# Weight splits of the first and last steps of a fused attention and GeGLU kernel placed elsewhere in the step order

## The chip, the cores and the metric

The kernel runs on one core of one Trainium2 chip, in one launch. Its time is the device time of that core in microseconds (us). Three runs of the kernel before took 1610.37, 1612.19 and 1613.04 us, with 1612.19 us as the median. Traces come from one profiled execution each.

## The reference

The input x has 2048 tokens of 576 elements. Two branches read it, and a gate of its own per token mixes them.

```python
x = A_x
g = _sigmoid((x * gate_w).sum(-1, keepdims=True))
a = _A_ref(x, A_wq, A_wk, A_wv, A_wo, A_beta)   # 32 heads of 18, 4 segments of 512 tokens
b = _B_ref(x, B_w_gate, B_w_up, B_w_down)       # (gelu(x @ w_gate) * (x @ w_up)) @ w_down
return g * a + (1 - g) * b
```

Branch A is attention with a compressive memory: within each segment of 512 tokens a causal softmax attention, mixed head by head with a read of a memory that the earlier segments wrote, and an output projection by wo (576 x 576). Branch B is a gated feed-forward layer with 4608 hidden units: w_gate and w_up are 576 x 4608, w_down is 4608 x 576. All of it is in float32.

## The kernel before

Every float32 product is made of fp16 matmuls: an operand is scaled by a power of two and split into a high half (a cast by ScalarE) and a low half (the operand minus its high half, by GpSimd or VectorE). Three products high-high, high-low and low-high stand for one.

The kernel has three stages. The first (to about 228 us of the profile) projects q, k and v, keeps the attention memory and writes q, k, v and the memory's result to DRAM. The second is a hand-made order of 72 steps, `step(v)` for v = 0 to 71, each about 18 us in the profile. The third adds the last down products and the output projection to the result, row block by row block.

A step has two jobs. Its own job is feed-forward work: step v treats hidden tile f = v // 2 (128 of the 4608 units) and token pair p = v % 2 (two of the four segments). With sums of weights and of inputs, kept as tiles pairg and xt, it forms gate and up products in few matmuls: `product` and `rest` (lines 1039, 1046 and 1051) accumulate in three PSUM banks named V (bank V), X (bank G) and Y (bank U). VectorE copies and adds between banks (L1141, L1144, L1176, L1195, L1203), ScalarE applies gelu (L1029), VectorE multiplies by the up value (`hidden`, L1021, which empties banks G and U), and ScalarE and GpSimd split the hidden value in two halves hh (L1025, L1026). Two tiles make a block fb = v // 4, and i4 = v % 4. The down products of block fb - 1 (`down`, L999, six matmuls and one VectorE accumulation L1005 or L1007) are spread over the four steps of block fb: eight chains per step, five early and three late. They take turns in two PSUM banks named dn. Block 0 (v = 0 to 3) has no down products to fill in; its first products are issued a step ahead instead.

The other job is attention. A unit is one head in one segment; scores of unit a go to banks st and dn (`scores`, L902), VectorE adds the mask and takes maxima (L910), ScalarE exponentiates (`powers`, L920, L923) and casts the high rows (`pair_rows`, L933), GpSimd forms the low rows (L934), and the DMA queue of SyncE transposes high and low rows (`turn_rows`, L940). `values` (L954) multiplies the transposed rows by v, and `normalize` follows. Attention lags by LAG = 2: step v scores units 2k and 2k + 1 with k = v - 2, and takes the values of two units of the step before. The transposed rows pt have two buffers, the values of a head one bank.

The weights of a coming tile are prepared beside this: loads of gate and up weights into one of three buffers raw (L196) and of down weights into one of two buffers rawd (L202), scaling on GpSimd (`scale_g`, L264, two pieces a tile; `scale_d`, L303), sums on GpSimd (`sums_g`, L285 to L289), and the split: `high_g(f, b)` on ScalarE (L295), `low_g(f, b)` on GpSimd (L299), with b = 0 before the sums and b = 1 after them, and `high_d`, `low_d` (L307, L311) for the down weights. From block 1 on `weights_first`, `weights_high` and `weights_low` place these; in block 0 single lines of `step` do.

At the end, from step LAST = 67 on, `finish(i)` prepares the output weights: i = 0 loads five pieces of wo, i = 1 takes their squares on ScalarE, i = 2 sums those on TensorE (L90, into a bank dn), derives the scale by short VectorE operations (L104, L97, L76, L77, L99, L100) and scales the gate (L1269), and i = 2, 3 and 4 split pieces 0 and 1, 2 and 3, and 4 (high half on ScalarE, L108; low half on VectorE, L111).

The order on TensorE, ScalarE, VectorE and GpSimd is the order in which the code issues instructions; each engine works through its own in turn and waits by semaphores. The order on SyncE's DMA queue is chosen by the framework; it too is worked through in turn, and a DMA that must wait for a buffer holds up those behind it.

Of the kernel before, what the change touches and what calls it, by code (L numbers as in the profile page):

```python
# [42 lines left out]
def kernel(ctx: ExitStack, tc: tile.TileContext, xs, wqk, wv, wo, wgu, wd, beta, out):  # L43
# [215 lines left out]
    def scale_g(f):  # L259
        if f >= NF:  # L260
            return
        for i in (1, 0):
            r = raw_g[f][:, i * KW : (i + 1) * KW]
            pool.tensor_scalar(r, r, scl[f // 2][0][:, 0:1], None, OP.mult)  # L264
# [26 lines left out]
    def high_g(f, b):  # L291
        if f < NF and not b:
            pair_g[f] = wts.tile([P, 2, GB * P], F16, name="pairg", tag="pairg", bufs=2)
        for p in parts_g(f, b):
            act.activation(spot(f, *p, 0), raw_g[f][:, p[0] : p[1]], AF.Copy)  # L295

    def low_g(f, b):
        for p in parts_g(f, b):
            pool.tensor_tensor(spot(f, *p, 1), raw_g[f][:, p[0] : p[1]], spot(f, *p, 0), OP.subtract)  # L299

    def scale_d(f):
        r = raw_d[f]
        pool.tensor_scalar(r, r, scl[f // 2 + 1][0][:, 1:2], None, OP.mult)  # L303

    def high_d(f):
        t = pair_d[f] = home["d"].tile([P, 2, D], F16, name="paird", tag="paird", bufs=4)
        act.activation(t[:, 0], raw_d[f], AF.Copy)  # L307

    def low_d(f):
        t = pair_d[f]  # L310
        pool.tensor_tensor(t[:, 1], raw_d.pop(f), t[:, 0], OP.subtract)  # L311
# [535 lines left out]
    with tc.tile_pool(name="keep", bufs=2, side="right", reuse_waits="tile") as kp, ExitStack() as tail:  # L847
# [270 lines left out]
        def step(v):  # L1118

            f, p = divmod(v, 2)  # L1120
            fb, i4 = divmod(v, 4)
            c, e = 2 * p, 2 * p + 1
            k = v - LAG
            on = lambda i: 0 <= i < 2 * H
# [6 lines left out]
            low = (k - 6) // 4 if i4 == 0 and 0 <= (k - 6) // 4 < H // 2 - 1 else None  # L1131
            x1, x2_, t = x16[c], x16[e], xt[p]
            end_pair()
            if v == 3:
                high_g(2, 1)
                low_g(2, 1)
            act_squares(v)
            V = ahead.pop(v) if v in ahead else first_product(v)
            X, Y = bank("G"), bank("U")
# [7 lines left out]
            if v == 1:  # L1147
                scale_result()
            some(fb - 1, early[:1])
            put(2 * k - 1, 1)  # L1150
            put(2 * k - 1, 2)
            puts.pop(2 * k - 1, None)
# [1 line left out]
                values(2 * k - 3)  # L1154
            weights_first(fb, i4)
            if v == 1:
                scale_d(0)
                scale_d(1)
            if on(k - 1):
                powers(2 * k - 1)  # L1160
                pair_rows(2 * k - 1, 0)
# [32 lines left out]
                puts[2 * k] = scores(2 * k)  # L1194
            dve.tensor_tensor(g1, Y, g1, OP.add)  # L1195
            gelu(f, e, g1, g1)
            if v == 3:
                for n in range(2):
                    high_d(n)
                    low_d(n)  # L1200
            put(2 * k, 2)
            if fb:
                dve.tensor_tensor(g0, V, g0, OP.add)  # L1203
                gelu(f, c, g0, g0)
            if on(k - 1) and fb:
                values(2 * k - 2)
            some(fb - 1, early[3:4])
            put(2 * k, 0)
# [6 lines left out]
                hidden(f, c, X, g0)  # L1215
                hidden_pair(f, c, g0)
            if v == 0:
                scale_g(2)
            if on(k):
                powers(2 * k)  # L1220
                pair_rows(2 * k, 0)
# [7 lines left out]
            if low is not None:  # L1229
                result_low(low)  # L1230
            some(fb - 1, late[1:])
            if on(k - 1) and not fb:
                values(2 * k - 2)
            if fb:
                low_rests(f, (X, U4, x1), (Y, UG, x2_))
# [20 lines left out]
        def finish(i):  # L1256

            if i == 0:
                for k in range(KT):
                    rows[k] = op_.tile([P, D], F32, name="wor", bufs=5)  # L1260
                    sp.dma_start(rows[k], wo[:, k])
            if i == 1:
                for k in range(KT):
                    wos[k] = op_.tile([P, 2, D], F16, name="wo", bufs=5)
                    act.activation(wos[k][:, 1].bitcast(BF16), rows[k], AF.Square, accum_out=wst[:, k : k + 1])
            if i == 2:
                scale_sum(2, wst[:, 0:5])

                dve.tensor_scalar(gate[:, 2], gate[:, 0], wis[:, 2:3], wis[:, 3:4], OP.mult, OP.mult)  # L1269
            if i >= 2:  # L1270
                for k in ((0, 1), (2, 3), (4,))[i - 2]:
                    pair_of(wos[k], rows[k], wsc[:, 2:3])

        LAG = 2
        LAST = 2 * H + LAG + 1
        with tc.manual_schedule(engines=ORDERED):
            for v in range(2 * NF):
                step(v)

                if v == LAST:  # L1280
                    atn.close()
                    op_ = tail.enter_context(tc.tile_pool(name="outp", bufs=2, side="right", reuse_waits="tile"))
                if v >= LAST:
                    turned(2 * (v - LAST))
                    turned(2 * (v - LAST) + 1)
                    finish(v - LAST)
            end_pair()
            turns.update(of=3)


            fb = NB - 1
            for t in range(10, 16):
                turned(t)
            for t in range(16):
                for n in range(2):
                    down(fb, t, n)
                for n in range(2):
                    o = bank("st", 2)
                    chain_x(o[:, :NH], lambda i: ot[t][:, i], lambda k, b: wos[k][:, b, n * NH : (n + 1) * NH])
                    av = acc[:, t, n * NH : (n + 1) * NH]  # L1300
                    dve.scalar_tensor_tensor(av, o[:, :NH], gate[:, 2, t : t + 1], av, OP.mult, OP.add)
                    if t == 15:
                        sp.dma_start(out[t * P :, n * NH : (n + 1) * NH], av)
                if t < 15:
                    sp.dma_start(out[t * P : (t + 1) * P, :], acc[:, t])
# [40 lines left out]
```

## Time and profile before

| | us |
|---|---|
| median of three timed runs | 1612.19 |
| lowest and highest run | 1610.37, 1613.04 |
| span of the profiled execution, first to last instruction | 1608.8 |
| TensorE (PE) busy | 1594.9 |
| ScalarE (ACT) busy | 1162.3 |
| VectorE (DVE) busy | 1141.2 |
| GpSimd (POOL) busy | 1132.9 |

The profiled execution is known by its span; the median of the timed runs is 3.4 us longer. Rows of a timeline read: start in us from the span's start, duration in us, engine, line, operation, output and input tiles with shapes, count, and in brackets the idle time of the engine before the instruction with what ended it. Rows of a group read: busy us and mean ns, then idle us before them. Rows by stretch read: length, then busy us (and instructions) of PE, PEld, DVE, ACT and POOL, the granted clock of TensorE, the busy share of the DMA engines and GB/s. Lines are those of the kernel before.

### The profile page before, as it was taken

To read this page: it belongs to the slowest core of one execution; us is meant where nothing else is said; L and a number is where in the kernel's file an instruction comes from. 1 tells how busy PE (TensorE), PEld (TensorE's weight loads), DVE (VectorE), ACT (ScalarE), POOL (GpSimd) and SP (SyncE) were. 2 spreads that over 40 slices of the span, in tenths; PEclk is the share of its full clock that TensorE was granted. 3 is DMA by queue.
4 is the path that set the end of the run, shared out by engine and by line. 5 is a ranking of instruction groups with operands and counts; after the bars stand their busy time and mean duration, and the time that the engine had idled before them with its cause. 6 is when DMAs were issued, how large, how long until landed. Compare 5 with 4: busy or idle time off the path is not lost.

```text
span 1608.8 us, 32608 instructions
## 1 busy us (share of the span) xinstructions
PE 1594.9 (99%) x11924; PEld 933.3 (58%) x11924; DVE 1141.2 (71%) x2938; ACT 1162.3 (72%) x1968; POOL 1132.9 (70%) x1093
## 2 busy tenths in 40 slices
PE   9999999999999999999999999999999999999999
PEld 6655754555555555555555555555555555555577
DVE  6575785677777777777777777777777777765543
ACT  6666446888888888888888888888888888863200
POOL 2233647798978888888978788887879787885200
PEclk9999999999999999999999999999999999999999
DMA  6532343788878788888987898878788797837251
GB/s 243 190 122 81 133 146 85 122 139 126 136 122 141 123 142 125 142 136 126 141 128 136 126 145 124 145 123 155 130 132 135 130 136 129 129 65 166 49 133 60
DMA packets 472016, 209.00 MB, mean 130 GB/s; under 512 B 427568, under 2 KB 437040, under 8 KB 471344
## 3 DMA queue, kind: packets, MB, share of 16 engines
q1 hardware_dynamic: 471856, 206.92, 71.1%
q8 instruction: 94, 1.54, 0.4%
q14 instruction: 66, 0.54, 0.1%
HBM read 90.99 MB, written 27.26 MB: 73 GB/s over the span
## 4 chain that ended last, share of the span: by engine, by line
PE 96%; DMA 1%; DVE 1%; POOL 1%; ACT 0%; issue 0%; SPq 0%; POOLq 0%; DVEq 0%
PE dn L999 26%; PE U L1039 17%; PE V L1039 12%; PE G L1039 11%; PE pv L954 4%; PE st L328 3%; PE st L318 3%; PE dn L328 2%; PE G L318 2%; PE U L1046 2%; PE st L902 2%; PE V L1051 1%; PE U L318 1%; PE G L1051 1%; PE V L1046 1%; PE G L1046 1%
## 5 line engine op out<-in xcount | busy, mean ns | idle before, releaser
L934 POOL TENSOR_TENSOR ph<-pf,ph 128x512 f16<-128x512 f32 (+1 forms) x256 | 354.0, 1404 | 177.8 <-ACT ph L933 175.9
L999 PE MATMUL dn<-paird,hh 128*128 128x288 f16 x3396 | 476.8, 286 | 0.9 <-POOL paird L311 0.9
L1039 PEld LDWEIGHTS <-pairg 128*128 128x128 f16 x3024 | 285.0, 98 | 312.6 <-issue 17.6
L999 PEld LDWEIGHTS <-hh 128*128 128x128 f16 x3456 | 332.3, 98 | 138.1 <-issue 2.6
L1007 DVE SCALAR_TENSOR_TENSOR acc<-dn,ev,acc 128x288 f32<-128x288 f32 x534 | 274.0, 516 | 95.9 <-PE dn L999 87.2
L923 ACT ACTIVATE pf<-pf,mb,esc 128x512 f32<-128x512 f32 (+3 forms) x512 | 292.9, 642 | 6.7
L1039 PE MATMUL G<-x,pairg 128*128 128x512 f16 x864 | 209.9, 379 | 4.0 <-DVE gl L1021 4.0
L1039 PE MATMUL U<-xt,pairg 128*128 128x512 f16 x864 | 210.0, 379 | 0.0
L1026 POOL TENSOR_TENSOR hh<-gl,hh 128x512 f16<-128x512 f32 x144 | 163.9, 1159 | 56.1 <-ACT hh L1025 56.1
L910 DVE CUSTOM_DVE_ANT_0 pf<-st,mask 128x512 f32<-128x512 f32 (+2 forms) x384 | 183.9, 504 | 0.0
L299 POOL TENSOR_TENSOR pairg<-raw,pairg 128x640 f16<-128x640 f32 (+2 forms) x144 | 173.9, 1230 | 10.6 <-ACT pairg L295 10.6
L933 ACT ACTIVATE ph<-pf 128x512 f16<-128x512 f32 (+1 forms) x256 | 172.4, 720 | 0.0
L1176 DVE COPY gl<-U 128x512 f32<-128x512 f32 x72 | 49.8, 691 | 135.6 <-PE U L1039 135.6
L295 ACT ACTIVATE pairg<-raw 128x640 f16<-128x640 f32 (+2 forms) x144 | 89.5, 648 | 69.9 <-POOL raw L289 40.7
L264 POOL TENSOR_SCALAR raw<-raw,sc 128x640 f32<-128x640 f32 x72 | 134.8, 1885 | 0.0
L1029 ACT ACTIVATE gl<-gl,sc 128x512 f32<-128x512 f32 x144 | 98.3, 717 | 45.9 <-DVE gl L1195 25.5
L1039 PE MATMUL V<-xt,pairg 128*128 128x512 f16 x432 | 105.7, 381 | 0.0
L1195 DVE TENSOR_TENSOR gl<-U,gl 128x512 f32<-128x512 f32 x72 | 49.7, 690 | 78.6 <-PE U L1051 71.3
L1039 PE MATMUL U<-x,pairg 128*128 128x512 f16 x432 | 105.0, 379 | 0.4 <-DVE gl L1195 0.4
L1039 PE MATMUL V<-x,pairg 128*128 128x512 f16 x432 | 104.8, 378 | 0.4 <-ACT hh L1025 0.2
L1025 ACT ACTIVATE hh<-gl 128x512 f16<-128x512 f32 x144 | 82.8, 616 | 24.9 <-DVE gl L1021 24.8
L920 ACT ACTIVATE mb<-mx,esc 128x4 f32<-128x4 f32 x128 | 37.8, 295 | 86.5 <-DVE mx L910 83.7
(268 smaller groups left out, 2566.6 us busy)
## 6 DMA issues: line engine op xcount, KB each, us to landing
raw<-in_wgu_dram SPq DMA_DIRECT2D x36, 640.0 KB
rawd<-in_wd_dram SPq DMA_DIRECT2D x36, 288.0 KB
qk<-stage SPq DMA_DIRECT2D x36, 256.0 KB
qt<-qk SPq DMA_DIRECT2D x128, 72.0 KB
kt<-qk SPq DMA_DIRECT2D x128, 72.0 KB
vp<-vstage SPq DMA_DIRECT2D x16, 296.0 KB
vt<-vp SPq DMA_DIRECT2D x16, 296.0 KB
qt<-qk SPq DMA_DIRECT2D x128, 36.0 KB
```

Source lines behind the costliest of these rows:

```text
L264: pool.tensor_scalar(r, r, scl[f // 2][0][:, 0:1], None, OP.mult)
L299: pool.tensor_tensor(spot(f, *p, 1), raw_g[f][:, p[0] : p[1]], spot(f, *p, 0), OP.subtract)
L318: pe.matmul(o, w(k, a), x[:, 4 * b + k], start=n == 0, stop=False)
L910: dve.tensor_tensor_reduce(prob[a][:, COL[qi] : COL[qi + 1]], ov, mask[:, L - (qi + 1) * P :], 1.0, -3e38, OP.add, OP.max, mx[a][:, qi : q ...
L923: act.activation(r, r, AF.Exp, bias=b[:, qi : qi + 1], scale=esc[:, 0, c : c + 1])
L933: act.activation(h[:, 0, cols], p[:, cols], AF.Copy)
L934: pool.tensor_tensor(h[:, 1, cols], p[:, cols], h[:, 0, cols], OP.subtract)
L999: pe.matmul(o[:, :NH], hh[:, a, q * P : (q + 1) * P], w[:, b, n * NH : (n + 1) * NH], start=i == 0, stop=i == 5)
L1007: dve.scalar_tensor_tensor(av, o[:, :NH], ev, av, OP.mult, OP.add)
L1026: pool.tensor_tensor(hh[:, 1], t, hh[:, 0], OP.subtract)
L1029: act.activation(t, o, AF.Gelu_apprx_tanh, scale=scl[f // 2][0][:, 2 + c : 3 + c])
L1039: pe.matmul(o, w[:, i, (a + k) * P : (a + k + 1) * P], x[:, b + k], start=start and k == 0 and i == 0 and b == h, stop=k == 1 and i == 1, ...
```

## The change

Five things are placed elsewhere; no computation is added or left out.

- The scaling of the first two down weight tiles (`scale_d(0)`, `scale_d(1)`) moves from v = 1 to the end of v = 0. Their splits (`high_d`, `low_d`) move from v = 3 to v = 1. The scaling of the third gate and up tile (`scale_g(2)`) moves from the end of v = 0 to v = 1, behind them.
- The second half of that tile's split (`high_g(2, 1)`, `low_g(2, 1)`) moves from the start of v = 3 to v = 2, behind the gelu of the second token segment.
- The even values of v = 4 (`values(2)`, of unit 2) move from behind the scores of unit 4 to behind the late down chains of the step. From v = 5 on they stay where they were.
- `finish(2)`, `finish(3)` and `finish(4)` move from the ends of v = 69, 70 and 71 to the same steps' first third, behind the first early down chain.

```diff
@@ step(v)
-            if v == 3:
-                high_g(2, 1)
-                low_g(2, 1)
             act_squares(v)
...
             some(fb - 1, early[:1])
+            if v >= LAST + 2:
+                finish(v - LAST)
             put(2 * k - 1, 1)
...
             if v == 1:
-                scale_d(0)
-                scale_d(1)
+                for n in range(2):
+                    high_d(n)
+                    low_d(n)
+                scale_g(2)
...
             gelu(f, e, g1, g1)
-            if v == 3:
-                for n in range(2):
-                    high_d(n)
-                    low_d(n)
+            if v == 2:
+                high_g(2, 1)
+                low_g(2, 1)
...
-            if on(k - 1) and fb:
+            if on(k - 1) and v > 4:
                 values(2 * k - 2)
...
             if v == 0:
-                scale_g(2)
+                scale_d(0)
+                scale_d(1)
...
-            if on(k - 1) and not fb:
+            if on(k - 1) and v <= 4:
                 values(2 * k - 2)
@@ behind step(v)
-                    finish(v - LAST)
+                    if v < LAST + 2:
+                        finish(v - LAST)
```

What this does to GpSimd's order in v = 0 and v = 1, from the split of the first hidden value on (raw is the third tile, rawd and paird the two down weight tiles). Before:

```order
L1026 TENSOR_TENSOR hh_2521<-gl,hh_2521 128x512
L264 TENSOR_SCALAR raw<-raw,sc 128x640 x2
L882 MEMSET ob 128x288
L1026 TENSOR_TENSOR hh_2550<-gl,hh_2550 128x512
L303 TENSOR_SCALAR rawd<-rawd,sc 128x576 x2
L1026 TENSOR_TENSOR hh_2621<-gl,hh_2621 128x512
```

And now:

```order
L1026 TENSOR_TENSOR hh_2521<-gl,hh_2521 128x512
L303 TENSOR_SCALAR rawd<-rawd,sc 128x576 x2
L882 MEMSET ob 128x288
L1026 TENSOR_TENSOR hh_2550<-gl,hh_2550 128x512
L311 TENSOR_TENSOR paird<-rawd,paird 128x576 x2
L264 TENSOR_SCALAR raw<-raw,sc 128x640 x2
L1026 TENSOR_TENSOR hh_2627<-gl,hh_2627 128x512
```

The scaling of the down weights has taken the place of that of the third tile, and the latter comes behind the down weights' low halves.

GpSimd's order in v = 2 and v = 3, from the last of the third tile's sums on (ph are the low rows of attention units 0 and 1, pairg the third tile's second half). Before:

```order
L289 TENSOR_TENSOR raw<-raw 128x128
L1026 TENSOR_TENSOR hh_2726<-gl,hh_2726 128x512
L934 TENSOR_TENSOR ph<-pf,ph 128x512
L934 TENSOR_TENSOR ph<-pf,ph 128x768
L1026 TENSOR_TENSOR hh_2771<-gl,hh_2771 128x512
L299 TENSOR_TENSOR pairg<-raw,pairg 128x640
L299 TENSOR_TENSOR pairg<-raw,pairg 128x512
L934 TENSOR_TENSOR ph<-pf,ph 128x512
L934 TENSOR_TENSOR ph<-pf,ph 128x768
L311 TENSOR_TENSOR paird<-rawd,paird 128x576 x2
L1026 TENSOR_TENSOR hh_2867<-gl,hh_2867 128x512
```

And now:

```order
L289 TENSOR_TENSOR raw<-raw 128x128
L299 TENSOR_TENSOR pairg<-raw,pairg 128x640
L299 TENSOR_TENSOR pairg<-raw,pairg 128x512
L1026 TENSOR_TENSOR hh_2736<-gl,hh_2736 128x512
L934 TENSOR_TENSOR ph<-pf,ph 128x512
L934 TENSOR_TENSOR ph<-pf,ph 128x768
L1026 TENSOR_TENSOR hh_2781<-gl,hh_2781 128x512
L934 TENSOR_TENSOR ph<-pf,ph 128x512
L934 TENSOR_TENSOR ph<-pf,ph 128x768
L1026 TENSOR_TENSOR hh_2867<-gl,hh_2867 128x512
```

Between the low rows of unit 0 and those of unit 1 only one hidden value is left, and none of the weights' low halves stand in v = 3. ScalarE's high halves have moved in the same way. On the DMA queue the load of the sixth tile, which needs the third tile's buffer, now stands ahead of the loads of head 2 and of the transposes of unit 0, where it stood behind the latter; the loads of the second pair of down weights stand some twenty places further ahead.

VectorE's order at v = 69. Before, from the last five down accumulations of the step to the two products that follow it:

```order
L1007 SCALAR_TENSOR_TENSOR acc<-dn,ev,acc 128x288 x5
L104 TENSOR_REDUCE sv<-dn 128x1
L97 TENSOR_SCALAR wz<-sv 128x1
L76 TENSOR_SCALAR va<-wz 128x1
L77 TENSOR_SCALAR va<-va 128x1
L99 TENSOR_SCALAR wsc<-va 128x1
L100 TENSOR_SCALAR wis<-va 128x1
L1269 TENSOR_SCALAR gate<-gate,wis 128x16
L111 SCALAR_TENSOR_TENSOR wo<-wor,wsc,wo 128x576 x2
L1021 SCALAR_TENSOR_TENSOR gl<-G,sc,gl 128x512
L1021 SCALAR_TENSOR_TENSOR gl<-U,sc,gl 128x512
```

And now, from the first early down chain's accumulation on (L1177 and L1270 are the former L1176 and L1269):

```order
L1007 SCALAR_TENSOR_TENSOR acc<-dn,ev,acc 128x288
L104 TENSOR_REDUCE sv<-dn 128x1
L97 TENSOR_SCALAR wz<-sv 128x1
L76 TENSOR_SCALAR va<-wz 128x1
L77 TENSOR_SCALAR va<-va 128x1
L99 TENSOR_SCALAR wsc<-va 128x1
L100 TENSOR_SCALAR wis<-va 128x1
L1270 TENSOR_SCALAR gate<-gate,wis 128x16
L111 SCALAR_TENSOR_TENSOR wo<-wor,wsc,wo 128x576 x2
L1177 COPY gl<-U 128x512
L1007 SCALAR_TENSOR_TENSOR acc<-dn,ev,acc 128x288
```

The chain of the output weights no longer stands ahead of the two L1021 that empty banks G and U for the next step, but ahead of the copy of bank U in the middle of its own.

## The prediction

> **What bounds the kernel now.** I read the page first, then the waits of TensorE, then TensorE's busy time by stretch, and only then the instructions of the two stretches that are not full.
>
> ```profile
> span 1608.8 us, 32608 instructions
> PE 1594.9 (99%) x11924; PEld 933.3 (58%) x11924; DVE 1141.2 (71%) x2938; ACT 1162.3 (72%) x1968; POOL 1132.9 (70%) x1093
> ```
>
> TensorE is occupied in all but 13.9 us of the span. The change removes no matmul, so it can only win what TensorE waits. The two longest waits of TensorE (total us, times, longest us):
>
> ```profile
> PE G L1039 <- DVE gl L1021: 4.0, 3, 2.7
> PE pv L954 <- DMA pt<-ph: 3.4, 4, 1.5
> ```
>
> The stretches say where they lie (us, then TensorE busy):
>
> ```profile
> 200.00:300.00 100.00, 94.89 (x537) 47.41 (x536) 67.20 (x156) 59.43 (x97) 61.82 (x57) 1.00 0.47 115
> 1450.00:1500.00 50.00, 46.98 (x279) 26.14 (x277) 28.94 (x60) 17.84 (x34) 23.38 (x26) 1.00 0.75 172
> ```
>
> 5.1 us are lost in the stretch of the steps v = 0 to 4, 3.0 us in that of v = 68 to 70: over half of the 13.9 us, and the places of the change. The granted clock (the third number from the end) is 1.00 in both rows.
>
> **The head: v = 3 and v = 4.** TensorE's own instructions, from the first product of v = 4 to that of v = 6:
>
> ```profile
> 275.08 1.47 PE L1039 MATMUL V<-xt,pairg 128*128 128x512 f16 x6
> 278.14 0.53 PE L999 MATMUL dn<-paird,hh 128*128 128x288 f16 x3 [0.17 <-POOL paird L311]
> 279.37 0.40 PE L999 MATMUL dn<-paird,hh 128*128 128x288 f16 x2 [0.71 <-POOL paird L311]
> 280.61 0.64 PE L954 MATMUL pv<-vt,pt 128*128 128x37 f16 x19 [0.81 <-DMA pt<-ph]
> 290.73 0.19 PE L954 MATMUL pv<-vt,pt 128*128 128x37 f16 x1 [1.53 <-DMA pt<-ph]
> 291.84 0.64 PE L954 MATMUL pv<-vt,pt 128*128 128x37 f16 x19 [0.92 <-DMA pt<-ph]
> 298.29 1.47 PE L1039 MATMUL V<-xt,pairg 128*128 128x512 f16 x6
> 316.78 1.47 PE L1039 MATMUL V<-xt,pairg 128*128 128x512 f16 x6
> ```
>
> Step v = 4 takes 298.29 - 275.08 = 23.21 us, step v = 5, which runs the same instructions, 18.49 us: v = 4 is 4.7 us too long. The named waits make 4.14 us of it: 0.88 for the low half of the first down weights (L311), 0.81 for the values of unit 1, 2.45 for those of unit 2.
>
> The rows that feed these waits: the group of L264 on the page (busy us, mean ns), then instructions of GpSimd, ScalarE and the DMA queue:
>
> ```profile
> L264 POOL TENSOR_SCALAR raw<-raw,sc 128x640 f32<-128x640 f32 x72 | 134.8, 1885 | 0.0
> ```
> ```profile
> 245.40 3.42 POOL L303 TENSOR_SCALAR rawd<-rawd,sc 128x576 f32<-128x576 f32 x2
> 259.36 0.45 POOL L289 TENSOR_TENSOR raw<-raw 128x128 f32<-128x128 f32 x1
> 271.27 2.53 POOL L299 TENSOR_TENSOR pairg<-raw,pairg 128x640 f16<-128x640 f32 x2
> 276.81 2.51 POOL L311 TENSOR_TENSOR paird<-rawd,paird 128x576 f16<-128x576 f32 x2 [0.30 <-ACT paird L307]
> ```
> ```profile
> 252.63 1.13 ACT L295 ACTIVATE pairg<-raw 128x640 f16<-128x640 f32 x2
> 262.41 0.63 ACT L1025 ACTIVATE hh<-gl 128x512 f16<-128x512 f32 x1 [1.58 <-DVE gl L1021]
> 268.51 1.24 ACT L295 ACTIVATE pairg<-raw 128x640 f16<-128x640 f32 x2
> 272.17 1.35 ACT L933 ACTIVATE ph<-pf 128x512 f16<-128x512 f32 x2
> ```
> ```profile
> 276.54 2.10 SPq L940 DMA_TRANSPOSE pt<-ph  x1
> ```
>
> *Down weights in v = 1.* Their scaling (3.42 us) moves to v = 0, and the low halves (2.51 us of GpSimd) now stand where it stood, at 245.40: they end near 247.9 us, 30 us before TensorE first uses them. The 0.88 us go, and would come back only if they were 30 us late. What they push is the scaling of the third tile, now behind them: two pieces of 1.885 us, done near 251.7. ScalarE takes that tile at 252.63. Margin 0.9 us, so I cost it at nothing; without it each us goes on to the next paragraph.
>
> *Third tile's second half in v = 2.* Its sums end at 259.36 + 0.45 = 259.8 us; ScalarE is then free from 260.8 to 262.4 (the 1.58 us of idle time quoted) and the two pieces take 1.24 us. They fit, with 1.0 us in hand. GpSimd follows after the first of the two for 2.5 us, to 264.1; its next piece could start at 262.41 + 0.63 = 263.0, so it comes 1 us later, hidden because ScalarE ends the high rows of unit 0 only shortly before the 268.51 quoted. What it frees is the start of v = 3: 1.24 us of ScalarE and 2.53 us of GpSimd no longer stand between the rows of unit 0 and those of unit 1. ScalarE's high rows of unit 1 start at 272.17 - 1.15 = 271.0, GpSimd follows after the first of the two, 0.7 us later, for about the 2.5 us of its other pairs, and the low transpose is issued at 274.2 to 274.7 in place of 276.54.
>
> *Values of unit 1.* That transpose was used at 280.61, 4.07 us after its issue. Issued at 274.7 it is there at 278.7. TensorE, without the waits named, asks for it at 280.61 - 0.81 - 0.88 = 278.9, or up to 0.5 us sooner, as the step's excess (4.7) is larger than its named waits (4.14). I keep 0.3 us of wait. The bounds: all of it goes (0), or the transposes keep their old time and 0.81 + 0.88 = 1.7 us stay, since TensorE merely arrives earlier.
>
> *Values of unit 2 at the end of v = 4.* They stood after the scores; the transpose landed 1.53 + 0.92 us too late. At the end of the step they come behind thirty more down matmuls and one product: what now lies between 292.4 and 298.29, over 5 us. TensorE came to them at 290.73 - 1.53 = 289.2; 2 us sooner and 5.2 us of work later is 292.4, so even the old landing of 291.84 is in time, and the rows are written about 2 us earlier. The 2.45 us go. The price is a half microsecond of cover lost before the fifth down chain, which shares a PSUM bank with the scores: I allow 0 to 0.3 us, taken as 0.1. The next transposes into that buffer are queued behind a load that waits for the later scores of the same step anyway, so the later read holds up nothing.
>
> *What is late next.* ScalarE gets less of the shortening than TensorE:
>
> ```profile
> 295.53 0.30 ACT L920 ACTIVATE mb<-mx,esc 128x4 f32<-128x4 f32 x1 [1.59 <-DVE mx L910]
> 314.03 0.30 ACT L920 ACTIVATE mb<-mx,esc 128x4 f32<-128x4 f32 x1 [1.26 <-DVE mx L910]
> ```
>
> It idles 1.59 us for the maxima of unit 4; those come some 5 us earlier, and by my chain it then runs 0.8 us behind TensorE. The 1.26 us of idle time one step on absorb this. Head: 4.7 - 0.3 - 0.1, taken as **4.4 us** (2.8 to 4.9).
>
> **The tail: v = 69 to 71.** First product and G product of three steps, and the third down chain of v = 69:
>
> ```profile
> 1472.38 1.47 PE L1039 MATMUL V<-xt,pairg 128*128 128x512 f16 x6
> 1473.68 1.46 PE L1039 MATMUL G<-x,pairg 128*128 128x512 f16 x6
> 1480.90 0.90 PE L999 MATMUL dn<-paird,hh 128*128 128x288 f16 x6
> 1489.45 1.46 PE L1039 MATMUL V<-xt,pairg 128*128 128x512 f16 x6
> 1493.65 1.46 PE L1039 MATMUL G<-x,pairg 128*128 128x512 f16 x6 [2.74 <-DVE gl L1021]
> 1509.04 1.47 PE L1039 MATMUL V<-xt,pairg 128*128 128x512 f16 x6
> 1511.52 1.46 PE L1039 MATMUL G<-x,pairg 128*128 128x512 f16 x6 [1.00 <-DVE gl L1021]
> ```
>
> G follows V by 1.30 us at v = 69, by 4.20 at v = 70 and 2.48 at v = 71: 2.90 + 1.18 = 4.1 us lost, because the output weights' chain on VectorE stands before the products that empty G. Now it stands behind the first down chain of its own step:
>
> ```profile
> 1478.79 0.69 DVE L1176 COPY gl<-U 128x512 f32<-128x512 f32 x1 [2.36 <-PE U L1039]
> 1489.63 0.16 DVE L104 TENSOR_REDUCE sv<-dn 128x1 f32<-128x5 f32 x1
> 1491.39 1.55 DVE L111 SCALAR_TENSOR_TENSOR wo<-wor,wsc,wo 128x576 f16<-128x576 f32 x2 [0.45 <-ACT wo L108]
> ```
>
> The chain lasts 1491.39 + 1.55 - 1489.63 = 3.3 us; the gap at v = 69 is 2.36 us, from 1476.4. The copy L1176 ends near 1480.4 and the down result behind it near 1480.9. TensorE's third down chain, at 1480.90, takes that bank; it comes near 1481.1 now, as the sums matmul precedes it. So 0.2 us are left, if the chain keeps its 3.3 us. It may not, since GpSimd forms sums there, four pieces of 0.72 us and one of 0.45 us, from 1476.31 to about 1479.9:
>
> ```profile
> 1476.31 0.72 POOL L285 TENSOR_TENSOR raw<-raw 128x256 f32<-128x256 f32 x1
> 200.38 1.27 POOL L477 TENSOR_TENSOR phi<-phi,expm 128x512 f32<-128x512 f32 x1
> ```
> ```profile
> 200.72 2.00 DVE L360 SCALAR_TENSOR_TENSOR xt<-acc,xsc,xt 128x1024 f16<-128x1024 f32 x1
> 231.03 1.27 DVE L368 SCALAR_TENSOR_TENSOR x<-acc,xsc,x 128x1024 f16<-128x1024 f32 x1
> ```
>
> The same form takes 1.27 us beside an idle GpSimd and 2.00 us when it starts 0.93 us before a GpSimd tensor_tensor ends. The low halves L111 have the same form. Held for up to one 0.72 us piece each, the two cost 1.4 us, of which 0.2 is in hand; if the short operations ahead of them are held too, I bound the wait at 2.0 us, since GpSimd is done by 1479.9. The ends are 0 and 2.0 us; I take 0.8 us, as both low halves meet a piece, but not each from its start. At v = 70 and 71 the pieces fit their gaps, as no long chain precedes them. Tail: 4.1 - 0.8 = **3.3 us** (2.1 to 4.1).
>
> [...]
>
> **The sum.** 4.4 + 3.3 = 7.7 us. Against the profile: 1608.8 - 7.7 = 1601.1 us of span. The median of the timed runs is 3.4 us above the span, so the time is 1612.19 - 7.7 = **1604.5 us**.
>
> **Rivals.**
> 1. *VectorE's chain is held in full at v = 69* (2.0 us of wait). For it: sums run all along the new place. Against: the short operations work on one element a partition, and no row shows such a one held. Gain 4.4 + 2.1: 1605.7 us. Chance 0.13.
> 2. *The transposes of unit 1 come no earlier.* The load of the sixth tile now goes out before those of unit 0 and may slow them. For it: 1.7 us stay at v = 4. Against: it leaves when GpSimd is done, near 264.1, and those rows are ready near 268. Gain 3.0 + 3.3: 1605.9 us. Chance 0.12.
> 3. *The change does not do what it says*: ScalarE, not TensorE, paces v = 4 to 6, and the head's 4.4 us come back as waits once the 0.8 us of lag exceed the 1.26 us of slack. Gain 3.3 us or less: 1608.9 us and above. Chance 0.10.
> 4. *Slower: the DMA queue blocks.* That load waits for GpSimd's third-tile halves and stands, in the queue, ahead of the transposes of unit 0. Its margin is between 0 and the 3.9 us from 264.1 to 268; each us of GpSimd's lateness beyond that delays the values of unit 0 and all behind them. It decides from 7.7 to 11.6 us of lateness; at 15 us the time is 1612.19 - 7.7 + 15 - 3.9 = 1615.6 us. Against: GpSimd would have to slip by more than all that moved past it (2.51 + 2.53 us). Chance 0.03.
>
> **The numbers.** 0.2% is 3.2 us, about what a measurement here can tell from no change. The forecast has 0.62. With the bounds (gain 4.9 to 9.0 us) it spans 1603.2 to 1607.3; the runs before differ by 1.8 us below and 0.9 us above their median, so the range is 1602.0 to 1608.3 and holds rivals 1 and 2. Rivals 3 and 4 lie outside. Faster by over 0.2%: 0.62 + 0.13 + 0.12, less 0.01 for noise, 0.86; within: 0.11; slower: 0.03.
>
> **What would show it.** Right: v = 4 lasts about 18.8 us, no wait for L311 at v = 4, the unit 2 values without a wait, G following V by 1.3 us at v = 70 and 71, and the pair of L111 longer than 1.55 us at v = 69 with a short wait of the third down chain. Wrong: transposes of unit 0 or 1 landing later than TensorE by over 1 us, a wait at v = 5 or 6 for ScalarE, or a wait of several us in v = 69. A gain under 3.2 us makes the forecast wrong.

## The result and the profile after

The changed kernel takes 1603.80 us (median of four runs, 1603.44 to 1605.29), the kernel before 1612.62 us beside it (four runs, 1610.37 to 1613.13): a ratio of 0.995, 95% interval 0.9935 to 0.9964. The forecast was 1604.5 us. The profiled execution took 1603.76 us, 1.8 us over its span.

The page of the changed kernel, span and TensorE's busy time:

```profile
span 1602.0 us, 32613 instructions
PE 1593.6 (99%) x11924; PEld 932.9 (58%) x11924; DVE 1142.2 (71%) x2938; ACT 1162.6 (73%) x1968; POOL 1136.7 (71%) x1093
```

TensorE is idle 8.4 us of the span, where it was 13.9 us before. Its longest waits now (total us, times, longest):

```profile
PE pv L954 <- DMA pt<-ph: 2.0, 3, 0.9
PE dn L999 <- DVE acc L1007: 0.3, 1, 0.3
PE G L1039 <- DVE gl L1021: 0.3, 1, 0.3
```

The 4.0 us of G for L1021 are 0.3, the 0.9 for L311 are gone, and the values wait 2.0 us in place of 3.4. By stretch, the two that were not full:

```profile
200.00:300.00 100.00, 97.19 (x570) 49.20 (x569) 70.24 (x164) 62.40 (x104) 64.64 (x60) 1.00 0.51 118
1450.00:1500.00 50.00, 49.39 (x292) 27.20 (x291) 34.38 (x63) 18.46 (x35) 24.48 (x25) 1.00 0.73 166
```

**The head.** TensorE's timeline from the values of unit 0 at the end of v = 3 to the first product of v = 5:

```profile
273.62 0.19 PE L954 MATMUL pv<-vt,pt 128*128 128x37 f16 x1 [0.29 <-DMA pt<-ph]
274.72 0.64 PE L954 MATMUL pv<-vt,pt 128*128 128x37 f16 x19 [0.91 <-DMA pt<-ph]
275.73 1.47 PE L1039 MATMUL V<-xt,pairg 128*128 128x512 f16 x6
279.06 0.18 PE L954 MATMUL pv<-vt,pt 128*128 128x37 f16 x1
280.07 0.64 PE L954 MATMUL pv<-vt,pt 128*128 128x37 f16 x19 [0.82 <-DMA pt<-ph]
293.94 0.66 PE L954 MATMUL pv<-vt,pt 128*128 128x37 f16 x20
295.18 1.47 PE L1039 MATMUL V<-xt,pairg 128*128 128x512 f16 x6
```

Step v = 4 lasts 295.18 - 275.73 = 19.45 us in place of 23.21: 3.76 us gained. The values of unit 2 no longer wait, nor do the down weights. But the values of unit 0, in the step ahead, wait 0.29 + 0.91 = 1.20 us, where they waited 0.18. The queue shows why (start, time on the queue):

```profile
263.54 0.34 SPq L196 DMA_DIRECT2D raw<-in_wgu_dram  x1
267.56 5.04 SPq L940 DMA_TRANSPOSE pt<-ph  x2
274.42 3.51 SPq L940 DMA_TRANSPOSE pt<-ph  x2
```

Before, the same three were:

```profile
268.11 3.57 SPq L940 DMA_TRANSPOSE pt<-ph  x2
273.82 0.38 SPq L196 DMA_DIRECT2D raw<-in_wgu_dram  x1
274.30 4.34 SPq L940 DMA_TRANSPOSE pt<-ph  x2
```

The 640 KB load of the sixth tile (L196) has moved from between the two pairs of transposes to a place ahead of both. The pair behind it, unit 0's, is on the queue for 5.04 us and not 3.57. GpSimd starts unit 1's low rows 2.6 us earlier (271.17 in place of 273.75), but the unit's transposes start only at 274.42, because those of unit 0 (until 272.60), and three small loads behind them (until 274.31), hold the queue.

**The tail.** First product (V), G product and third down chain, v = 69 to 71:

```profile
1469.23 1.47 PE L1039 MATMUL V<-xt,pairg 128*128 128x512 f16 x6
1470.53 1.46 PE L1039 MATMUL G<-x,pairg 128*128 128x512 f16 x6
1478.39 0.90 PE L999 MATMUL dn<-paird,hh 128*128 128x288 f16 x6 [0.34 <-DVE acc L1007]
1486.69 1.47 PE L1039 MATMUL V<-xt,pairg 128*128 128x512 f16 x6
1488.00 1.46 PE L1039 MATMUL G<-x,pairg 128*128 128x512 f16 x6
1503.39 1.47 PE L1039 MATMUL V<-xt,pairg 128*128 128x512 f16 x6
1504.70 1.46 PE L1039 MATMUL G<-x,pairg 128*128 128x512 f16 x6
```

G follows V by 1.30 to 1.31 us in all three steps. v = 70 falls from 19.59 to 16.70 us from V to V, v = 71 gives back 2.48 - 1.31 = 1.17 us, and v = 69 grows from 17.07 to 17.46: 2.89 + 1.17 - 0.39 = 3.7 us.

By the two traces the gain is thus: head 3.76, less 1.20 us by which v = 3 grew (V to V, 15.37 to 16.57) = 2.6; tail 3.7; and about 0.5 us that lie ahead of v = 3: its first product starts at 259.16 us in place of 259.71. In the traces of the kernels below it starts between 258.87 and 259.29 where weights are moved in v = 0 to 2, and between 259.11 and 259.49 where they are not. The two ranges overlap, so this is scatter at least in part, and no run shows that the change has a share in it. That makes the 6.8 us between the spans. The medians lie 8.8 us apart. Where the other 2 us are is what the experiments had to find.

### The profile page after: what moved, and what is told of

Its sections match the earlier page's. It is cut to its first block, busy times and chain, and to the rows that moved or that the text cites. A ratio compares the mean times of both kernels' runs of the same rounds, so it can differ in the third digit from the quotient of the medians.

```text
span 1602.0 us, 32613 instructions
## 1 busy us (share of the span) xinstructions
PE 1593.6 (99%) x11924; PEld 932.9 (58%) x11924; DVE 1142.2 (71%) x2938; ACT 1162.6 (73%) x1968; POOL 1136.7 (71%) x1093
## 3 DMA queue, kind: packets, MB, share of 16 engines
q8 instruction: 94, 1.54, 0.4%
## 4 chain that ended last, share of the span: by engine, by line
PE 94%; ACT 2%; DMA 1%; DVE 1%; SPq 1%; issue 0%; DVEq 0%
PE dn L999 26%; PE U L1039 17%; PE V L1039 12%; PE G L1039 11%; PE pv L954 4%; PE st L328 3%; PE st L318 2%; PE U L1046 2%; PE dn L328 2%; PE st L902 2%; PE G L318 1%; PE V L1051 1%; PE G L1051 1%; PE U L318 1%; PE V L1046 1%; PE G L1046 1%
## 5 line engine op out<-in xcount | busy, mean ns | idle before, releaser
L299 POOL TENSOR_TENSOR pairg<-raw,pairg 128x640 f16<-128x640 f32 (+2 forms) x144 | 174.1, 1231 | 12.3 <-ACT pairg L295 12.3
L1177 DVE COPY gl<-U 128x512 f32<-128x512 f32 x72 | 49.8, 691 | 130.2 <-PE U L1039 130.2
```

## The experiments

**The tail alone.** Kernel before, with the weight split of the output in mid-step only:

```diff
             some(fb - 1, early[:1])
+            if v >= LAST + 2:
+                finish(v - LAST)
...
-                    finish(v - LAST)
+                    if v < LAST + 2:
+                        finish(v - LAST)
```

> Only the output weights' move to mid-step in v = 69 to 71; the head as before. Theory (as in the changed kernel's trace: G follows V by 1.3 us in all three steps, and VectorE, held beside GpSimd's sums, makes the third down chain of v = 69 wait about 0.5 us): 4.1 - 0.5 = 3.6 us less, 1608.6 to 1609.0 us. Rival 1 of the prediction (held in full, 2.0 us of wait): 2.1 us less, about 1610.4 us. If the tail's gain were hidden by something later, no change.

Measured: 1608.02 us (10 runs) beside 1612.25, ratio 0.9974 (0.9964 to 0.9983): 4.2 us. The trace of this kernel has the same 0.33 us of wait at the third down chain, so rival 1 (held in full, 2.0 us) is out. The gain is somewhat over the 3.6 expected.

**The head alone.** The changed kernel with `finish` where it was before:

```diff
             some(fb - 1, early[:1])
-            if v >= LAST + 2:
-                finish(v - LAST)
...
-                    if v < LAST + 2:
-                        finish(v - LAST)
+                    finish(v - LAST)
```

> Only the moves in v = 0 to 4; the output weights as before. The prediction's sum says 4.4 us less (about 1608.0 us). The trace of the changed kernel says 2.6 us, or 3.1 us with the 0.55 us that its trace is ahead before the head begins (1609.1 to 1609.8 us). Rival 3 (ScalarE paces v = 4 to 6): no change. The values of unit 0 should wait about 1.2 us here too if the cause lies in the head.

Measured: 1608.64 us (11 runs) beside 1612.25, ratio 0.9977 (0.9968 to 0.9986): 3.6 us, between the prediction's 4.4 and the trace's 2.6. The two halves add up to 7.8 us of 8.8, and the intervals are too wide to show that one depends on the other. The values of unit 0 waited here as in the whole change, so that cost belongs to the head. Rival 3 (ScalarE paces) is out.

**The values of unit 2 alone**, on the kernel before:

```diff
-            if on(k - 1) and fb:
+            if on(k - 1) and v > 4:
                 values(2 * k - 2)
...
-            if on(k - 1) and not fb:
+            if on(k - 1) and v <= 4:
                 values(2 * k - 2)
```

> Only the values of unit 2 put at the end of v = 4; weights, tail and the order of the loads as before. Theory: the 2.45 us that TensorE waited for these rows go, 0 to 0.3 us come back at the chains behind them: 2.2 to 2.45 us less, about 1610.0 us, v = 4 lasts about 20.8 us, and the values of unit 0 keep their 0.18 us of wait. Rival 3 (ScalarE paces the steps behind): v = 5 or v = 6 gets longer than 18.49 us by what v = 4 loses, and the time does not change.

Measured: 1612.27 us beside 1612.25, ratio 0.9999 (0.999 to 1.0007). Both theories missed: v = 4 lasted 24.55 us, not 20.8, and v = 5 its normal 18.49 us, so nothing was handed on to ScalarE. The values of unit 2 did not wait. But those of unit 1 did, for 2.5 us, with the same program ahead of them that made them wait 0.81 us in the trace of before, and then the products ran slowly:

```profile
281.12 0.19 PE L954 MATMUL pv<-vt,pt 128*128 128x37 f16 x1 [1.56 <-DMA pt<-ph]
282.27 0.64 PE L954 MATMUL pv<-vt,pt 128*128 128x37 f16 x19 [0.96 <-DMA pt<-ph]
282.76 2.07 PE L1039 MATMUL V<-x,pairg 128*128 128x512 f16 x6
285.05 2.36 PE L1039 MATMUL U<-xt,pairg 128*128 128x512 f16 x6
287.99 1.46 PE L1039 MATMUL G<-x,pairg 128*128 128x512 f16 x6
```
```profile
284.00:286.00 2.00, 2.00 (x6) 0.70 (x5) 0.00 (x0) 0.32 (x1) 2.00 (x3) 0.50 0.43 150
```

Six matmuls that take 1.46 us elsewhere took 2.07 and 2.36, and the stretch in the second fence has a granted clock of 0.50 (the third number from the end): after the wait the clock fell to half. The trace of before has for the same two products:

```profile
281.10 1.46 PE L1039 MATMUL V<-x,pairg 128*128 128x512 f16 x6
284.63 1.46 PE L1039 MATMUL G<-x,pairg 128*128 128x512 f16 x6
```

From the one to the other it is 287.99 - 282.76 = 5.23 us with the fall, and 3.53 us without: the fall cost 1.70 us. Why the time did not change although unit 2 no longer waits, the next run shows.

**The kernel before again**, to see whether its profile was typical:

> The kernel before once more, unchanged, with a profile of its own. Theory (its time varies with whether TensorE's granted clock falls after the waits in v = 4 and v = 70, and with how late the transposes of unit 1 land): the profile of before showed neither fall; this one shows at least one stretch near 280 to 288 us or 1490 to 1500 us with a granted clock under 0.9, and is longer by 1.5 to 1.8 us for each, or the wait for unit 1 is over the 0.81 us shown. Rival: it repeats the profile of before, 1608.8 us of span with a clock of 1.00 throughout.

Measured: 1613.18 us in one run, span 1611.5, against 1608.8 in the profile from which the prediction was made. Stretches of this second trace (the third number from the end is the granted clock):

```profile
284.00:288.00 4.00, 4.00 (x17) 1.76 (x15) 1.00 (x2) 2.92 (x8) 4.00 (x4) 0.67 1.30 100
1492.00:1496.00 4.00, 1.41 (x5) 0.54 (x5) 3.47 (x5) 2.22 (x4) 0.66 (x1) 0.87 0.95 197
1496.00:1500.00 4.00, 4.00 (x17) 1.95 (x16) 1.22 (x2) 0.65 (x1) 3.31 (x3) 0.71 0.63 165
```

And the same stretches in the trace of before that the prediction used:

```profile
284.00:288.00 4.00, 4.00 (x26) 2.29 (x24) 3.19 (x8) 3.84 (x10) 4.00 (x3) 1.00 1.22 80
1492.00:1496.00 4.00, 2.35 (x14) 1.36 (x14) 3.67 (x7) 1.28 (x3) 1.60 (x2) 1.00 0.90 162
1496.00:1500.00 4.00, 4.00 (x23) 2.06 (x21) 1.59 (x3) 0.68 (x1) 3.20 (x3) 1.00 0.49 140
```

The same program has a full clock in both places in the one execution, and a fall in each in the other. The tail's price, at v = 70 in the second trace of before:

```profile
1490.39 1.46 PE L1039 MATMUL V<-xt,pairg 128*128 128x512 f16 x6
1494.59 2.40 PE L1039 MATMUL G<-x,pairg 128*128 128x512 f16 x6 [2.75 <-DVE gl L1021]
1501.84 1.46 PE L1039 MATMUL G<-x,pairg 128*128 128x512 f16 x6
```

In the first trace of before, the G product stood at 1493.65, and the next one here:

```profile
1499.22 1.46 PE L1039 MATMUL G<-x,pairg 128*128 128x512 f16 x6
```

G waits 2.74 to 2.75 us in both, but the way to the next G product is 1501.84 - 1494.59 = 7.25 us here and 1499.22 - 1493.65 = 5.57 us there: 1.68 us. The change removes the long waits, and with them most of the falls. (One of its four runs took 1605.29 us at a mean granted clock of 0.999, the others 1603.44 to 1603.85 at 1.000; that looks like one fall left, but no trace of that run is kept.) So its gain is larger in most executions than in the pair of traces. The first profile of before was a quick execution: a span of 1608.8 us is a time of about 1610.5, and of the 50 executions of that kernel timed beside the experiments three took 1610.6 us or less. Span against span, this second trace lies 1611.5 - 1602.0 = 9.5 us above the changed kernel, the first 6.8; the medians' 8.8 lie between. It also fits the 4.2 us of the tail alone, where its rows give 3.6. From the first product of v = 3 to that of v = 5 the changed kernel is 3.84 us shorter than this second trace and 2.56 shorter than the first; the 3.6 us of the head alone lie between.

The head of the second trace of before answers for the values of unit 2. Unit 1 waits 1.13 + 0.95 = 2.08 us there and the clock falls, so TensorE comes late to unit 2, which then waits only this:

```profile
292.81 0.65 PE L954 MATMUL pv<-vt,pt 128*128 128x37 f16 x19 [0.66 <-DMA pt<-ph]
```

From V to V its v = 4 lasts 299.26 - 274.43 = 24.83 us, and with the values of unit 2 alone 24.55: 0.3 us. The 2.45 us of the prediction stood in a trace in which unit 1 was quick.

**The sixth tile's load behind the transposes.** The changed kernel, in which a one-column write by GpSimd ties the load to its place:

```diff
     def load_g(f):
         if f < NF:
             raw_g[f] = raw_tile()
+            if f == 5:
+                pool.memset(raw_g[f][:, 0:1], 0.0)
...
-                load_g(n0 + 5)
+                if fb:
+                    load_g(n0 + 5)
...
                 turn_rows(2 * k - 1)
+            if v == 3:
+                load_g(5)
```

> The changed kernel, with one difference: the sixth tile's load of 640 KB is asked for in v = 3 after the low rows of unit 1 (a one-column write by GpSimd into its buffer ties it to that place), so it stands in the DMA queue behind the transposes of units 0 and 1 and not ahead of both. Theory (the load ahead of them slows the transposes): the two waits of TensorE for the values of unit 0 (1.2 us) and unit 1 (0.8 us) shrink to 0.2 us and at most 0.4 us, the time falls by 1.0 to 1.4 us against the changed kernel, to 1602.4 to 1602.8 us. Rival (the transposes are late for their own length, or for the rows that they read): both waits stay, 1603.8 us.

Measured: 1602.22 us (five runs, 1601.68 to 1602.52), ratio to before 0.9938 (0.9925 to 0.995), 1.6 us under the changed kernel. TensorE and the queue:

```profile
273.07 0.66 PE L956 MATMUL pv<-vt,pt 128*128 128x37 f16 x20
277.99 0.64 PE L956 MATMUL pv<-vt,pt 128*128 128x37 f16 x19 [0.38 <-DMA pt<-ph]
```
```profile
267.47 3.37 SPq L942 DMA_TRANSPOSE pt<-ph  x2
272.16 3.76 SPq L942 DMA_TRANSPOSE pt<-ph  x2
276.02 0.54 SPq L198 DMA_DIRECT2D raw<-in_wgu_dram  x1
```

Unit 0 does not wait, unit 1 waits 0.38 us, and the transposes of unit 0 are on the queue for 3.37 us. As expected: the load ahead of them was the cause.

**The same load moved in the kernel before**, nothing else of the change (the diff is the one just shown):

> The kernel before, with one difference: the sixth tile's load stands behind the transposes of units 0 and 1. Theory (a 640 KB load ahead of a transposition makes it late, and a long wait lowers TensorE's granted clock for some us): the second transposition of unit 1 keeps its start near 276.5 us, since its rows come no earlier, but lands within 4 us; the values of unit 1 wait at most 0.8 us, not the 2.1 to 2.5 us of the two kernels with this head (output weights alone, values alone), the granted clock stays at 1.00 between 280 and 290 us, and the time is 1 to 3 us under that before (1609.3 to 1611.2 us). Rival (the rows are the limit, not the load): no change, and the clock falls in 280 to 290 us as in those two.

Measured: 1610.77 us (11 runs) beside 1612.73, ratio 0.9989 (0.998 to 0.9998). The values of unit 1 did not wait at all:

```profile
279.02 0.96 PE L956 MATMUL pv<-vt,pt 128*128 128x37 f16 x20
```

Their second transposition started 1.77 us after the first product of v = 4, against 1.46 in the first trace of before, so their rows came no earlier: the load explains their whole wait. The clock stayed at 1.00 between 280 and 290 us, as expected. What the expectation did not foresee came right behind: the wait moved to unit 2 (1.36 + 0.94 us), and the fall with it, with a clock of 0.62 between 292 and 296 us.

**The third tile's second half back at v = 3**, in the changed kernel:

```diff
-            if v == 2:
-                high_g(2, 1)
-                low_g(2, 1)
...
             end_pair()
+            if v == 3:
+                high_g(2, 1)
+                low_g(2, 1)
```

> The changed kernel with the third tile's second half back at the start of v = 3. The sixth tile's load then goes out after the transposes of unit 0 and ahead of those of unit 1, as before the change. Theory: the values of unit 0 lose their 1.2 us of wait, those of unit 1 get 1.7 to 2.5 us in place of 0.8 us, as their rows come 2.5 us later behind a load: 0.5 to 2.2 us slower than the changed kernel, 1604.3 to 1606.0 us, or up to 1.7 us more where the clock falls. Rival 2 of the prediction (the move gains nothing at unit 1): 1602.6 to 1603.8 us.

Measured: 1605.35 us (five runs, 1603.80 to 1605.70), ratio 0.9953 (0.994 to 0.9965); a repeat of the changed kernel on the same chip (next) took 1604.04 (1603.70 to 1605.50). The runs overlap, so a difference of 1.3 us is not settled by them. The trace shows what was expected: unit 0 waits 0.19 us, unit 1 0.88 + 0.95 = 1.83 us, and then the clock falls:

```profile
278.85 0.19 PE L954 MATMUL pv<-vt,pt 128*128 128x37 f16 x1 [0.88 <-DMA pt<-ph]
280.00 0.68 PE L954 MATMUL pv<-vt,pt 128*128 128x37 f16 x19 [0.95 <-DMA pt<-ph]
```
```profile
282.00:284.00 2.00, 2.00 (x6) 0.68 (x5) 0.00 (x0) 1.94 (x5) 2.00 (x3) 0.54 0.27 84
```

From the first product of v = 3 to that of v = 5 it is 37.68 us here and 36.02 in the changed kernel. The difference, 1.66 us, is the price of one fall: what the move gains at unit 1 it loses at unit 0. The runs fit that: two took 1603.80 and 1604.00 us at a mean granted clock of 1.000, three 1605.35 to 1605.70 at 0.999.

**GpSimd's sums later at v = 69.** The sums of the last pair were written behind the second down chain, in the changed kernel and in the one with the load behind.

```diff
-            if i4 == 1 and fb:
+            if i4 == 1 and 0 < fb < NB - 1:
                 sums_g(n0 + 1)
...
-            if fb:
+            if fb and v != LAST + 2:
                 weights_high(fb, i4)
                 weights_low(fb, i4)
...
             some(fb - 1, early[1:2])
+            if v == LAST + 2:
+                sums_g(2 * fb + 1)
+                weights_high(fb, i4)
+                weights_low(fb, i4)
```

> The changed kernel; at v = 69 GpSimd's sums of the last pair, and the halves that follow them, stand behind the second down chain and not beside VectorE's low halves. Theory (GpSimd holds VectorE): the pair of L111 falls from 2.36 us to 1.55 us, the gate's scaling L1270 from 0.52 to 0.29 us, the third down chain's wait of 0.34 us goes, and v = 69 loses about 0.5 us (17.46 us from V to V now): 1603.3 us. Rival (the chain is as long without GpSimd): L111 stays at 2.36 us and nothing changes. If the halves come too late for v = 70, its first product waits, by up to 1 us.

> The changed kernel with both: the sixth tile's load behind the transposes of units 0 and 1, and the sums of v = 69 behind the second down chain. If the two are independent, 1602.2 - 0.5 = 1601.7 us; if the second is worth nothing, 1602.2 us.

This experiment did not do what it was for. GpSimd has no other instruction between the two places, so its order did not change: the sums ran at the same time, and L111 took 2.36 and 2.37 us. The two are repeats of kernels already measured, 1604.04 us for the changed kernel and 1601.86 us (one run of five at 1605.48) with the load behind.

**GpSimd's sums earlier.** With the load behind, the sums now stand at the end of v = 68, ahead of the low halves of the hidden rows:

```diff
-            if i4 == 1 and fb:
+            if i4 == 1 and 0 < fb < NB - 1:
                 sums_g(n0 + 1)
...
             ends.append((f, e, Y, g1))
+            if v == LAST + 1:
+                sums_g(2 * fb + 1)
```

> The changed kernel with the sixth tile's load behind the transposes of units 0 and 1, and with GpSimd's sums of the last pair at the end of v = 68, ahead of the low halves of the hidden rows, where GpSimd idles 8.2 us, and not beside VectorE's output weights at v = 69. Theory (GpSimd holds VectorE): the pair of L111 at v = 69 falls from 2.36 us to 1.55 us, the gate's scaling from 0.52 to 0.29 us, the third down chain's wait of 0.34 us goes, v = 69 lasts 16.95 to 17.1 us from V to V in place of 17.46, and the time is about 0.4 us under 1602.2 us (1601.6 to 1602.0). Rival (the chain is as long without GpSimd beside it): L111 stays at 2.36 us, the wait stays, 1602.2 us.

Measured: 1601.13 us (five runs, 1600.84 to 1601.97), ratio 0.9932 (0.992 to 0.9945), the lowest time of all kernels here. VectorE at v = 69, first in the changed kernel, then with the sums earlier:

```profile
1474.94 2.36 DVE L111 SCALAR_TENSOR_TENSOR wo<-wor,wsc,wo 128x576 f16<-128x576 f32 x2 [0.23 <-DMA orow<-oa]
1478.44 1.45 DVE L224 TENSOR_SCALAR z<-x,z 128x4 f32<-128x4 f32 x1
```
```profile
1472.69 1.55 DVE L111 SCALAR_TENSOR_TENSOR wo<-wor,wsc,wo 128x576 f16<-128x576 f32 x2 [0.45 <-DMA orow<-oa]
1475.38 0.23 DVE L226 TENSOR_SCALAR z<-x,z 128x4 f32<-128x4 f32 x1
```

The pair of L111 is back at 1.55 us, the third down chain no longer waits, and v = 69 lasts 16.97 us from V to V in place of 17.46. GpSimd beside VectorE was the cause of the half microsecond.

**Down weights back** (their split in v = 3, their scaling in v = 1, the third tile's in v = 0, as before the change), and **values of unit 2 back** behind the scores, each in the changed kernel; the diffs are those of the change, reversed.

> The changed kernel with the first down weights' split back in v = 3 and their scaling back in v = 1. The prediction's sum: the 0.88 us of L311 come back, 1604.7 us. Theory by the trace of the changed kernel: they lie ahead of the 0.82 us that the values of unit 1 wait there, so they are hidden in it, 1603.8 to 1604.2 us, with a longer wait for L311 and a shorter one for unit 1.

> The changed kernel with the values of unit 2 back behind the scores in v = 4. The prediction's sum: 2.45 - 0.1 = 2.35 us come back, 1606.2 us. Theory by the trace of the changed kernel: TensorE asks for them near 287 us and the second transposition lands near 289.6 to 290 us, so 2.2 to 2.8 us come back, and up to 1.7 us more where the granted clock falls after the wait: 1606.0 to 1608.3 us. Rival (as values alone on the kernel before, which moved nothing): 1603.8 us.

Measured, on the same chip: 1603.72 us (1603.60 to 1603.91) for the first, 1605.20 us (1604.43 to 1605.60) for the second. The down weights were worth nothing on top of the rest. The reason was another than the one on record: their chain did not wait at all. GpSimd's instruction in the trace with the down weights back:

```profile
275.24 2.51 POOL L311 TENSOR_TENSOR paird<-rawd,paird 128x576 f16<-128x576 f32 x2 [1.19 <-ACT paird L307]
```

It stood at 276.81 before the change, and comes 1.6 us earlier because the third tile's half no longer stands ahead of it in v = 3. So the two moves remove the same 0.88 us, and either is enough: with the third tile put back and the down weights left in v = 1 (above), no wait for L311 appears either. The values of unit 2, put back, wait 0.83 us until 289.42, and v = 4 lasts 20.58 us in place of 19.45: they are worth 1.1 us by the trace, 1.2 to 1.4 us by the medians (1605.20 against 1603.80 for the changed kernel and 1604.04 for its repeat), and not 2.35, since the rows of unit 2 come earlier with the rest of the change.

## Why the prediction was right, point by point

- **What bounds the kernel.** Right: TensorE's waits in two stretches. In the trace it is idle 5.5 us less (13.9 to 8.4); the rest of the 6.8 us between the spans is in its busy time (1594.9 to 1593.6).
- **Down weights in v = 1.** Their wait went, as foreseen, but it was not this edit that was needed for it: 0.88 us were credited to it, and with the third tile moved it is worth nothing.
- **Third tile's second half in v = 2.** Right in its times (ScalarE's pieces at 260.19, GpSimd done by 263.5) and in what it frees. Wrong in what was left out: GpSimd's end also releases the sixth tile's load, which the prediction knew only as rival 2, at unit 1, with 0.12. It struck unit 0 for 1.0 us more than before, and kept unit 1 at 0.82 us where 0.3 was allowed. The argument against it was the load's lead over the transposes, put at 3.9 us (264.1 to 268); the lead was 4.0 us (263.54 to 267.56), and they were slowed all the same. The wait of 1.20 us at unit 0 is one of the prediction's own signs of being wrong (over 1 us).
- **Values of unit 2.** Right: no wait, and the early chains took 0.13 us longer (1.76 against 1.63). Its size depended on the other parts: 1.1 to 1.4 us with them, nothing that could be measured without them.
- **What is late next.** ScalarE did not fall behind TensorE: it still idles 1.37 us for the maxima of unit 4, until 292.19, and 1.47 us one step on. The 0.8 us of lag that the chain gave was too much.
- **The head's sum** was mis-sized: 4.4 us, and 2.6 by the two traces (3.6 by the medians with the head alone). Of the 1.8 us, 1.2 are the growth of v = 3 (1.0 of it the longer wait of unit 0) and 0.5 are unit 1, both from the load: with the load behind, v = 3 and v = 4 together are 1.97 us shorter. The terms as written make 4.7 - 0.3 - 0.1 = 4.3 and not 4.4, and the lower end of the range would by its own terms be 1603.2 - 1.8 = 1601.4 us and not 1602.0; neither slip matters for the result.
- **Tail.** Right in its mechanism: G after V by 1.3 us, the pair of L111 at 2.36 us, a short wait of the third down chain. The wait was taken as 0.8 us and is 0.34 (v = 69 grew by 0.39), so the tail gave 3.7, not 3.3. "At v = 70 and 71 the pieces fit their gaps" holds, though L111 was longer at v = 70 too (1.94 us for two, beside GpSimd's L303, and 1.54 before the change). That both low halves are held for a full piece of GpSimd's, 1.4 us in all, was an estimate from the 2.00 against 1.27 us of one form; with 0.2 us in hand it would be a wait of 1.2 us where 0.34 was measured. That VectorE is held beside the sums is shown: the pair took 2.36 us there and 1.55 us with the sums earlier. But when the two low halves began (1474.94 and 1476.03), GpSimd's pieces had only 0.55 and 0.66 us to run, and the pair grew by 0.81 us in place of 1.4.
- **From the span to the time.** This step failed, and in the other direction. The sum set the median 3.4 us above the span. But time and span lie 1.7 to 1.8 us apart in the profiled executions whose own time is listed; the rest of the 3.4 was that the profiled execution was a quick one, without a fall of the clock. Those falls (1.7 us each) are part of what the change removes. So a gain of 7.7 was forecast, the traces show 6.8, the medians 8.8: the time came out within 0.7 us by luck, since the main errors cancel, the load in the head (1.8 us too much) and the clock in both places (2 us too little).
- **Rivals.** Rival 2's mechanism happened, at another place and a smaller price; rivals 1, 3 and 4 did not.

## What to carry to other kernels

Ask of every edit that ends an engine's work sooner which transfer that end releases, and what stands behind it in the queue: here a load that nobody waited for cost 1.6 us, and a one-column write that held it back won that again. Price a long wait of TensorE with the slow matmuls that can follow it (1.68 to 1.70 us here), and profile the kernel before more than once, since one execution may show none of them. Where two edits remove the same wait, credit it once.

## What was not expected of the hardware

- **The clock after a wait.** A wait of TensorE of about 1.8 to 2.7 us was followed in some executions by a lower granted clock that cost 1.68 to 1.70 us (5.23 against 3.53 us in the head, 7.25 against 5.57 in the tail). With the values alone the clock was 0.87, 0.50 and 0.78 in the three stretches of 2 us from 282 us on, and 1.00 in each of them in the first trace of before. At 0.50 a cost of 1.70 us makes some 3.4 us at the lower clock, by estimate. Of five traces with the 2.74 us wait at v = 70, three show the fall (output weights as before: values alone, head alone, the kernel before again; 0.67 to 0.71 in the lowest stretch of 4 us) and two do not (the kernel before, the load alone; 1.00). In the head, the values of one unit waited 1.83, 2.08, 2.09, 2.30 and 2.52 us in all, in two parts with a short matmul between, ahead of a fall (third tile back, the kernel before again, output weights alone, the load alone, values alone); 2.45 us in the first trace of before and 1.20 us in the changed kernel were followed by none. So the length of the wait alone does not decide: 1.83 us came ahead of a fall, and 2.74 us twice did not. What decides, no run shows.
- **A load ahead of transposes.** The transposes of unit 0 were on the queue 3.36 to 3.98 us in the kernels where the 640 KB load came later, and 4.86 to 5.04 us in those where it stood ahead of them with five small loads between. With the load directly ahead, the values of unit 1 could run 5.5 us after the first product of v = 4 in the first trace of before and with the third tile back, and 7.0, 7.3 and 7.8 us after it in the three others with the head of before (output weights alone, the kernel before again, values alone). With the load behind them, they ran within 4.9 us and waited 0.38 us at most. So the load goes with both a delay and a scatter of over 2 us; what makes the scatter, no run shows.
- **Short VectorE instructions beside GpSimd.** The prediction doubted that short operations are held. One-element ones were not (0.14 to 0.15 us each at v = 69, beside the sums and with the sums earlier), but L224, 128x4, took 1.45 us beside a GpSimd tensor_tensor (L299), and 0.23 us in the trace of before, with GpSimd idle. With the sums earlier it started at 1475.38, about where one GpSimd piece ended and the next began, and took 0.23 us (L226 there); the next instruction, 128x2, took 1.13 us. GpSimd is held as well: its sums L288 and L289 took 1.12 and 0.97 us beside L111 in the changed kernel, and 0.73 and 0.45 us in the median of the 36 of each in the trace of before.
